# Forming T by pairs of 64-row matmuls in two PSUM banks, with the recurrence on the common bank pool

## The chip, the cores and the metric

One core of a Trainium2 chip. The metric is the device time of one launch in microseconds (us). Each call to the chip also ran the kernel before, so its median differs a little from call to call (1780.7 to 1785.0 us).

## The reference, cut to what matters

Two rounds of attention with a recurrent memory, each followed by a gated feed-forward layer. The sequence is cut into 64 segments of 32 tokens; each segment attends to itself and to 8 memory rows, and the memory of the next segment is the attention's output at those rows. So the 64 segments are a chain. B = 1, model width 448, 16 heads of 256.

```python
for s in range(n_seg):                       # 64 segments of 32
    h = jnp.concatenate([mem, xs], axis=1)   # 8 memory rows + 32 tokens
    q, k, v = h @ Wq, h @ Wk, h @ Wv         # (einsums over the heads, cut)
    p = _softmax(jnp.where(mask, q @ k * scale, -1e9))
    o = (p @ v) @ Wo
    mem = o[:, :M, :]
    outs.append(o[:, M:, :])
```

## The kernel before

Wq and Wk are merged ahead of time into one matrix M per head, so the scores are h · M · hᵀ. In every step the kernel forms T = Mᵀ · hᵀ: 56 blocks of 128 outputs, each a product over K = 448, which is 3.5 times the 128 rows that one matmul takes (128*128 in the page below). The kernel pads the last half with zeros and makes four passes. The two layers of the model run in one step, four segments apart, so a matmul of T has 2 x 40 = 80 columns. There are 68 steps; the first and last four have one layer and 40 columns.

```python
POOLS = {"R": [0, 1, 2, 3, 5]}               # bank 4 accumulates N and W_down, 6 and 7 belong to the recurrence

def t_unit(self, t, c, u0, m):               # a unit: m = 4, 5 or 6 blocks in one PSUM bank
    ...
    R = S.tile("R", 1)
    def mms():
        b = R.b()
        return [MM(b[:, j * n:j * n + n], S.M[:, kt, 16 * c + u0 + j, :],
                   S.hT[:, pp, s, kt, l0:l1, :].rearrange("p l x -> p (l x)"), start=(kt == 0), stop=(kt == 3))
                for j in range(m) for kt in range(4)]
    ...                                      # then copies of the bank to TTm (memory rows) and TTs (segment rows)

def s_mem(self, t):                          # memory scores: first step of the recurrence
    b = S.bC[0]                              # bank 6, fixed
    ...

class _Order:                                # a list scheduler fixes the order on all engines at build time
    ...
    if e == "pe" and o.mode != mode:         # it charges a change of array tiling 95 ns
        c += 95.0
```

The chain of a step is T, memory scores, softmax, P transposed, U, the product with N, and the new memory into hT. Behind it, segment scores (s_seg), U of the segment (u_seg, matmuls `PTs,hK`), the product with N (`Nw,big`) and the feed-forward layer (`xBT,big`, `big,hB`) fill TensorE.

## Time and profile before

| | before |
|---|---|
| median of the first 3 runs | 1780.73 us (1775.98 to 1781.08) |
| TensorE busy | 96% |
| T | 15232 matmuls, 546 us busy |
| granted TensorE clock, mean | 0.989 |

The groups by form split T into its two widths:

```profile
L127 PE MATMUL b<-hT,Mw 128*128 128x80 bf16 x13440 | 496.5, 202 | 3.6 <-DVE hT L685 3.6
...
L127 PE MATMUL b<-hT,Mw 128*128 128x40 bf16 x1792 | 49.5, 183 | 1.3 <-DVE hT L685 1.0 <-issue 0.3
```

The timeline of TensorE (start us, duration us, instruction, count, and in brackets the idle time before it) shows T as one block:

```profile
907.09 0.92 PE L127 MATMUL b<-Nw,big 128*128 128x448 bf16 x4
907.84 8.19 PE L127 MATMUL b<-hT,Mw 128*128 128x80 bf16 x224
915.87 0.92 PE L127 MATMUL b<-Nw,big 128*128 128x448 bf16 x4
...
928.55 0.17 PE L127 MATMUL b<-selm,lo 128*128 128x16 bf16 x1
929.20 0.36 PE L127 MATMUL b<-hi,seln 128*128 128x448 bf16 x1 [0.48 <-ACT hT L684]
```

224 matmuls take 8.19 us, 36 ns from start to start, and nothing in the block waits. The pause of 0.48 us before `hi,seln` is the recurrence waiting for ScalarE to empty bank 6. In two long windows of the steady state (us, then busy time of each engine, and the clock as PEclk):

```profile
100.00:900.00 800.00, 776.49 (x14338) 567.85 (x14335) 486.49 (x1384) 321.40 (x910) 33.59 (x61) 1.00 0.02 5
900.00:1700.00 800.00, 776.93 (x13901) 564.11 (x13899) 477.37 (x1341) 323.72 (x911) 35.61 (x64) 0.99 0.02 4
```

### The profile page before, as it was taken

The page shows a single profiled execution, that of the slowest core. Times are in us where ns is not written, and L with a number is a line of the kernel's source. Part 1 is how long each engine was busy: PE and PEld are TensorE (multiplying, and loading weights), DVE is VectorE, ACT ScalarE, POOL GpSimd, SP SyncE. Part 2 cuts the span into 40 slices and gives each one's busy share as a digit, 9 for nine tenths or more (in the row PEclk, how much of TensorE's full clock was granted, in tenths as well). Part 3 has the DMA queues.
Part 4 walks back from the last instruction along what each step waited for, and adds up shares of the span by engine and source line. Part 5 has one row for each costly group of instructions (what it writes and reads, how often), then busy time and mean ns, then how long its engine had stood idle before and what let it go on. Part 6 is the DMA issues. An engine that isn't in the chain of part 4 may idle for free.

```text
span 1780.3 us, 67770 instructions
## 1 busy us (share of the span) xinstructions
PE 1700.7 (96%) x30612; PEld 1226.7 (69%) x30612; DVE 1073.2 (60%) x3058; ACT 720.6 (40%) x2031; POOL 91.0 (5%) x156
## 2 busy tenths in 40 slices
PE   6899999999999999999999999999999999999997
PEld 2566766777677667767766776776677677667765
DVE  7647565565656556565655656565665656566554
ACT  5433433444443334444333444334344433434432
POOL 3000000000000000000000000000000000000000
PEclk9999999999999999999999999999999999999999
DMA  9700000000000000000000000000000000000000
GB/s 227 219 4 4 4 5 5 4 5 5 5 4 5 5 4 5 5 5 4 5 5 4 5 5 5 4 5 4 4 5 6 5 4 5 3 3 4 4 4 5
DMA packets 55760, 27.52 MB, mean 15 GB/s; under 512 B 44584, under 2 KB 54576, under 8 KB 55472
## 3 DMA queue, kind: packets, MB, share of 16 engines
q1 hardware_dynamic: 55120, 22.94, 5.3%
q8 instruction: 241, 3.95, 0.9%
q14 instruction: 47, 0.39, 0.1%
q10 hardware_dynamic: 352, 0.24, 0.1%
HBM read 10.33 MB, written 1.84 MB: 7 GB/s over the span
## 4 chain that ended last, share of the span: by engine, by line
PE 75%; DVE 6%; ACT 2%; issue 1%; DVEq 0%
PE b L127 75%; ACT big L684 1%; DVE big L685 1%; DVE stat L714 1%; DVE TTs L685 1%; DVE xn L721 1%; ACT hT L684 1%; DVE ys L1015 1%; DVE XA L1008 1%; DVE XB L968 0%; DVE Es L843 0%; DVE stat L842 0%; DVE TTm L685 0%; DVE hT L685 0%; DVE part L957 0%
## 5 line engine op out<-in xcount | busy, mean ns | idle before, releaser
L127 PEld LDWEIGHTS b<-hT,Mw 128*128 128x128 bf16 x15232 | 539.8, 100 | 25.3 <-DVE hT L685 11.2
L127 PE MATMUL b<-hT,Mw 128*128 128x80 bf16 (+1 forms) x15232 | 546.0, 200 | 5.0 <-DVE hT L685 4.6
L127 PE MATMUL b<-Nw,big 128*128 128x448 bf16 (+1 forms) x1936 | 394.9, 358 | 8.2 <-DVE big L685 5.6
L685 DVE CAST TTs<-b 128x320 bf16<-128x320 f32 (+5 forms) x574 | 261.3, 455 | 78.6 <-PE b L127 78.3
L127 PEld LDWEIGHTS b<-Nw,big 128*128 128x128 bf16 (+1 forms) x1936 | 163.7, 100 | 157.1 <-issue 21.5
L127 PE MATMUL b<-xBT,big 128*128 128x128 bf16 (+1 forms) x3808 | 219.6, 217 | 0.7 <-ACT xBT L684 0.7
L685 DVE CAST TTm<-b 128x80 bf16<-128x80 f32 (+5 forms) x580 | 134.7, 232 | 129.5 <-PE b L127 98.0
L127 PEld LDWEIGHTS b<-xBT,big 128*128 128x128 bf16 x3808 | 204.7, 98 | 2.4 <-ACT xBT L684 0.9
L127 PE MATMUL b<-Nw,UTm 128*32 128x448 bf16 x3752 | 192.0, 356 | 0.6 <-ACT UTm L684 0.6
L685 DVE CAST big<-b 128x512 bf16<-128x512 f32 (+1 forms) x190 | 121.3, 659 | 103.9 <-PE b L127 102.8
L684 ACT ACTIVATE big<-b 128x512 bf16<-128x512 f32 (+1 forms) x322 | 153.7, 525 | 48.2 <-PE b L127 45.0
L127 PEld LDWEIGHTS b<-Nw,UTm 128*32 128x32 bf16 x3752 | 95.2, 97 | 88.9 <-issue 18.7
L685 POOL COPY hK<-xn 32x448 bf16<-32x448 bf16 x136 | 75.6, 556 | 1521.6 <-DVE xn L721 1470.4
L684 ACT ACTIVATE TTs<-b 64x256 bf16<-64x256 f32 (+5 forms) x310 | 127.6, 412 | 29.6 <-PE b L127 22.4
L995 ACT ACTIVATE gT<-b 128x256 bf16<-128x256 f32 x226 | 86.4, 382 | 128.8 <-PE b L127 124.1
L684 ACT ACTIVATE TTm<-b 64x64 bf16<-64x64 f32 (+4 forms) x304 | 69.4, 228 | 159.4 <-PE b L127 152.5
L996 DVE TENSOR_TENSOR hB<-gT,b 128x256 bf16<-128x256 bf16 x226 | 93.6, 415 | 64.8 <-ACT gT L995 54.0
L896 ACT ACTIVATE hi<-b 128x448 bf16<-128x448 f32 x67 | 36.5, 544 | 193.7 <-PE b L127 193.5
L897 DVE TENSOR_TENSOR lo<-b,hi 128x448 bf16<-128x448 f32 x67 | 41.4, 619 | 121.2 <-ACT hi L896 121.2
L127 PE MATMUL b<-big,hB 128*128 128x448 bf16 (+1 forms) x476 | 107.3, 355 | 0.0
L684 ACT ACTIVATE hK<-b 8x448 bf16<-8x448 f32 x94 | 50.4, 536 | 122.5 <-PE b L127 121.0
L127 PE MATMUL b<-PTs,hK 40*128 40x512 bf16 (+1 forms) x640 | 86.4, 348 | 13.3 <-DVE XA L1008 7.1
(103 smaller groups left out, 1396.1 us busy)
## 6 DMA issues: line engine op xcount, KB each, us to landing
big<-in_A_Wo_dram SPq DMA_DIRECT2D x3, 896.0 KB, 5.8
out_dram<-ys SPq DMA_DIRECT2D x32, 56.0 KB, 1.9
big<-in_B_W_down_dram SPq DMA_DIRECT2D x1, 1568.0 KB, 6.8
XA<-in_A_x_dram SPq DMA_DIRECT2D x28, 56.0 KB, 2.0
big<-in_B_W_up_dram SPq DMA_DIRECT2D x1, 1344.0 KB, 8.1
big<-in_B_W_gate_dram SPq DMA_DIRECT2D x1, 1344.0 KB, 8.5
Nw<-in_A_Wo_dram SPq DMA_DIRECT2D x1, 896.0 KB, 6.4
XA<-in_A_x_dram ACTq DMA_DIRECT2D x4, 56.0 KB, 4.3
```

What stands on the lines that cost most here:

```text
L127: ins = E.matmul(out, lhsT=lhsT, rhs=rhs, **kw)
L684: return E.activation(out(), src(), ACT.Copy)
L685: return E.tensor_copy(out(), src())
L714: S.dve(lambda E: E.bn_stats(st[:, so:so + 6], x), D, rd, [(key, 0)])
L721: S.dve(lambda E, a=a, b=b, src=src: E.tensor_scalar(S.xn[:, i, a:b], src, st[:, so + 6:so + 7], st[:, so + 8:so + 9], op0=ALU.subtract, o ...
L896: S.act(lambda E: E.activation(S.hi[:, :], b[:, 0:D], ACT.Copy), D, S.ps(6), [("hi",)])
L897: S.dve(lambda E: E.tensor_tensor(S.lo[:, :], b[:, 0:D], S.hi[:, :], ALU.subtract), D, S.ps(6) + [("hi",)], [("lo",)])
L995: S.act(lambda E, k=k, R=R, n=n: E.activation(S.gT[:, k % 2, 0:n], R[0].b()[:, 0:n], ACT.Relu), n, R[0].res(), [("gT", k % 2)])
L996: S.dve(lambda E, k=k, R=R, n=n, fcs=fcs: E.tensor_tensor(S.hB[:, fcs[0]:fcs[-1] + 1, 0:w], S.gT[:, k % 2, 0:n].rearrange("p (a b) -> p a ...
L1008: S.dve(lambda E: E.tensor_tensor(S.XA[64:128, q % 4, :], S.bO[0:64, 0:D], S.XB[0:64, p % 2, :], ALU.add), D, S.ps(4, half=(0,)) + xb, [(" ...
L1015: S.dve(lambda E: E.tensor_tensor(S.ys[64:128, p % 2, :], S.bO[64:128, 0:D], S.XB[64:128, p % 2, :], ALU.add), D, S.ps(4, half=(1,)) + xb, ...
```

## The change

Intent: the last half pass wastes half of the array. Two blocks, A and B, are formed together in two banks. Matmuls of 64 rows run as pairs, the upper half of the array on one bank, the lower half on the other: in a first part the upper halves of A's passes beside the lower halves of B's, and A's last half beside B's; in a second part the halves exchange banks. That is seven pairs for two blocks, 3.5 passes per block. A wait on TensorE's own counter keeps the second part from meeting the first in the same bank. Such pairs need more banks, so the recurrence gives up banks 6 and 7, and everything except bank 4 comes from one pool of seven.

```diff
-    POOLS = {"R": [0, 1, 2, 3, 5]}
+    POOLS = {"R": [0, 1, 2, 3, 5, 6, 7]}
...
-        self.M = self.sb("Mw", [128, 4, NO, 128])
+        self.M = self.sb("Mw", [128, 3, NO, 128])
+        self.M3 = self.sb("M3", [128, NO // 2, 128])
...
+                for j in range(m):
+                    v = slice(j * n, j * n + n)
+                    if not second:
+                        for kt in range(3):
+                            out.append(MM(a[:, v], S.M[top, kt, oa + j, :], mov(kt, top), start=(j == kt == 0), stop=False))
+                            out.append(MM(b[:, v], S.M[bot, kt, ob + j, :], mov(kt, bot), start=(j == kt == 0), stop=False))
+                        out.append(MM(a[:, v], S.M3[top, slot0 + j, :], mov(3, top), start=False, stop=False))
+                        out.append(MM(b[:, v], S.M3[bot, slot0 + j, :], mov(3, bot), start=False, stop=False))
+                    else:
+                        for kt in range(3):
+                            e = j == m - 1 and kt == 2
+                            out.append(MM(b[:, v], S.M[top, kt, ob + j, :], mov(kt, top), start=False, stop=e))
+                            out.append(MM(a[:, v], S.M[bot, kt, oa + j, :], mov(kt, bot), start=False, stop=e))
...
+            S.mm(mms, (3 if second else 4) * m * S.pitch(n), rd + rd2 if second else rd,
+                 R[0].res() + R[1].res() + (...), mode=1)
...
-        b = S.bC[0]
+        C = S.tile("R", 1)                   # s_mem, and likewise p_t_mem, u_mem, un_mem, m_t, m_nat
```

More of the change, by code (lines that the diff above doesn't have):

```diff
@@ L119, in pe @@
         waits = self._need("pe", reads, writes)
+        done = max([self.lastw[r][1] for r in reads if r[0] == "done"], default=0)
+        if self.known["pe"].get("pe", 0) < done:
+            self.known["pe"]["pe"] = done
+            waits.append((ev.sem, done))
         ev.n += 1
@@ L432, in alloc @@
         self.banks = [b[:, :] for b in bank]
-        self.bO, self.bC = bank[4], bank[6:8]
+        self.bO = bank[4]
     @staticmethod
@@ L547, in setup @@
         S.dve(lambda E: E.tensor_scalar(S.ident[:, :], cf[:, 0:128], 0.0, None, op0=ALU.is_equal), 128, [("Sm",)], [("ident",)])
-        S.pool(lambda E: E.memset(S.M[64:128, 3, 0:28, :], 0.0), 1800, (), [("Mz", 0)])
-        S.dve(lambda E: E.memset(S.M[64:128, 3, 28:56, :], 0.0), 1800, (), [("Mz", 1)])
         for j in range(4):
@@ L599, in setup @@
                 u, r = i + 8 * odd, slice(64 * odd, 64 * odd + 64)
-                S.cp(lambda u=u: S.M[0:64, 3, u:48:16, :], lambda T=T, r=r: T.b()[r, 0:384].rearrange("p (c x) -> p c x", c=3), 384,
-                     T.res(half=(odd,)), [("M", 3, u)])
-                S.cp(lambda i=i, odd=odd: S.M[0:64, 3, 48 + i, 64 * odd:64 * odd + 64], lambda T=T, r=r: T.b()[r, 384:448], 64,
-                     T.res(half=(odd,)), [("M", 3, 48 + i, odd)])
-        S.Mkeys = [("M", kt, u) for kt in range(4) for u in range(16)] + [("M", kt, 48 + i, o) for kt in range(4) for i in range(8) for o in range(2)]
-        S.Mkeys += [("Mz", 0), ("Mz", 1)]
+                for c in range(4):
+                    side, slot = S.PLACE[16 * c + (u if c < 3 else i)]
+                    d, w, x = 64 * side, (128 if c < 3 else 64), (64 * odd if c == 3 else 0)
+                    S.cp(lambda d=d, w=w, x=x, slot=slot: S.M3[d:d + 64, slot, x:x + w],
+                         lambda T=T, r=r, c=c, w=w: T.b()[r, 128 * c:128 * c + w], w, T.res(half=(odd,)), [("M3", c, u)])
+        S.Mkeys = [("M", kt, u) for kt in range(3) for u in range(16)] + [("M", kt, 48 + i, o) for kt in range(3) for i in range(8) for o in range(2)]
+        S.Mkeys += [("M3", c, u) for c in range(4) for u in range(16)]
         S.Nkeys = [("N", o) for o in range(NO)]
@@ L751, in ln_b, with t_pass @@
         S.cp(lambda: S.xBT[:, :, :].rearrange("p a b -> p (a b)"), lambda: T.b().bitcast(BF)[:, 0:512], 512, T.res(), [("xBT",)])
-    def t_unit(self, t, c, u0, m):
+    def t_pass(self, t):
         S = self
@@ L760, in t_unit @@
         n = nl * KEYS
-        R = S.tile("R", 1)
-        def mms():
-            b = R.b()
-            return [MM(b[:, j * n:j * n + n], S.M[:, kt, 16 * c + u0 + j, :],
-                       S.hT[:, pp, s, kt, l0:l1, :].rearrange("p l x -> p (l x)"), start=(kt == 0), stop=(kt == 3))
-                    for j in range(m) for kt in range(4)]
-        rd = [("hTx", pp, s)] + S.mkeys(pp, s, l0, l1)
-        if t == 0:
-            rd = rd + S.Mkeys
-        dst = [(nm, c, u0, half) for nm in ("TTm", "TTs") for half in ((0, 1) if c == 3 else (0,))]
@@ L773, in t_unit, with part, mms @@
-        S.mm(mms, 4 * m * S.pitch(n), rd, R.res() + dst)
-        src = lambda: R.b()[:, 0:m * n].rearrange("p (o l x) -> p o l x", o=m, l=nl)
+        rd = [("hTx", pp, s)] + S.mkeys(pp, s, l0, l1) + (S.Mkeys if t == 0 else [])
+        top, bot = slice(0, 64), slice(64, 128)
+        mov = lambda kt, h: S.hT[h, pp, s, kt, l0:l1, :].rearrange("p l x -> p (l x)")
+        keys = lambda c, u0: [(nm, c, u0, half) for nm in ("TTm", "TTs") for half in ((0, 1) if c == 3 else (0,))]
+        def part(g, R, second):
+            A, B = S.PAIRS[g]
+            m = A[2]
+            slot0 = sum(x[0][2] for x in S.PAIRS[:g])
+            oa, ob = 16 * A[0] + A[1], 16 * B[0] + B[1]
+            def mms():
+                a, b = R[0].b(), R[1].b()
+                out = []
+                for j in range(m):
[11 more added lines that the diff above has]
+                            out.append(MM(a[:, v], S.M[bot, kt, oa + j, :], mov(kt, bot), start=False, stop=e))
+                return out
+            rd2 = [("done", g)]
+            S.mm(mms, (3 if second else 4) * m * S.pitch(n), rd + rd2 if second else rd,
+                 R[0].res() + R[1].res() + ([("order",)] if second else keys(*A[:2]) + keys(*B[:2]) + [("done", g), ("order",)]), mode=1)
+            if second:
+                for k, T in zip((A, B), R):
+                    S.t_copies(t, T, *k)
@@ L775, in t_unit, with t_copies @@
+        R = []
+        for g in range(len(S.PAIRS)):
+            R.append([S.tile("R", 1), S.tile("R", 1)])
+            part(g, R[g], False)
+            if g:
+                part(g - 1, R[g - 1], True)
+        g = len(S.PAIRS) - 1
+        part(g, R[g], True)
+    def t_copies(self, t, R, c, u0, m):
+        S = self
+        l0, l1 = S.layers(t)
+        nl = l1 - l0
+        src = lambda: R.b()[:, 0:m * nl * KEYS].rearrange("p (o l x) -> p o l x", o=m, l=nl)
         for half in ((0, 1) if c == 3 else (0,)):
@@ L784, in t_unit @@
                  lambda h=h: src()[h, :, :, 0:SEG], m * nl * SEG, rr + z, [("TTs", c, u0, half)])
-    UNITS = [(3, 0, 4), (3, 4, 4)] + [(c, u, m) for c in range(3) for u, m in ((0, 6), (6, 5), (11, 5))]
-    TKEYS = [(c, u, half) for c, u, m in UNITS for half in ((0, 1) if c == 3 else (0,))]
+    PAIRS = [((3, 0, 4), (3, 4, 4)), ((0, 0, 6), (1, 0, 6)), ((0, 6, 5), (0, 11, 5)), ((1, 6, 5), (1, 11, 5)), ((2, 6, 5), (2, 11, 5)),
+             ((2, 0, 3), (2, 3, 3))]
+    TKEYS = [(k[0], k[1], half) for pair in PAIRS for k in pair for half in ((0, 1) if k[0] == 3 else (0,))]
+    PLACE = {}
+    for _a, _b in PAIRS:
+        for _j in range(_a[2]):
+            PLACE[16 * _a[0] + _a[1] + _j] = (0, len(PLACE) // 2)
+            PLACE[16 * _b[0] + _b[1] + _j] = (1, (len(PLACE) - 1) // 2)
     def s_mem(self, t):
@@ L793, in s_mem @@
         nl = l1 - l0
-        b = S.bC[0]
-        S.mm(lambda: [MM(b[:, l * KEYS:l * KEYS + KEYS], S.TTm[:, c, l, :], S.hT[:, pp, s, c, l, :], start=(c == 3), stop=(c == 2))
+        C = S.tile("R", 1)
+        S.mm(lambda: [MM(C.b()[:, l * KEYS:l * KEYS + KEYS], S.TTm[:, c, l, :], S.hT[:, pp, s, c, l, :], start=(c == 3), stop=(c == 2))
                       for l in range(l0, l1) for c in (3, 0, 1, 2)], 100.0 * nl,
-             [("TTm",) + k for k in S.TKEYS] + [("hTx", pp, s)] + S.mkeys(pp, s, l0, l1), S.ps(6))
+             [("TTm",) + k for k in S.TKEYS] + [("hTx", pp, s)] + S.mkeys(pp, s, l0, l1), C.res())
         st = S.stat
-        src = b[:, l0 * KEYS:l1 * KEYS].rearrange("p (l x) -> p l x", l=nl)
+        src = lambda: C.b()[:, l0 * KEYS:l1 * KEYS].rearrange("p (l x) -> p l x", l=nl)
         bc = lambda a: st[:, a:a + nl].unsqueeze(2).to_broadcast([128, nl, KEYS])
@@ L802, in s_mem @@
         n = nl * KEYS
-        S.dve(lambda E: E.tensor_reduce(st[:, 32:32 + nl], src, AX.X, ALU.max), n, S.ps(6), [("sm", 0)])
-        S.dve(lambda E: E.tensor_tensor(Em, src, bc(32), ALU.subtract), n, S.ps(6) + [("sm", 0)], [("Em",)])
+        S.dve(lambda E: E.tensor_reduce(st[:, 32:32 + nl], src(), AX.X, ALU.max), n, C.res(), [("sm", 0)])
+        S.dve(lambda E: E.tensor_tensor(Em, src(), bc(32), ALU.subtract), n, C.res() + [("sm", 0)], [("Em",)])
         S.act(lambda E: E.activation(Fm, Em, ACT.Exp, scale=SCALE), n, [("Em",)], [("Fm",)])
@@ L857, in p_t_mem @@
         S = self
-        pT = S.bC[1][:, :].bitcast(BF)
-        S.mm(lambda: [MM(pT[:, 0:128], S.Pm[:, :], S.ident[:, :], is_transpose=True)], 60.0, [("Pm",), ("ident",)], S.ps(7))
-        S.cp(lambda: S.PTm[:, :], lambda: pT[:, 0:128], 128, S.ps(7), [("PTm",)])
+        C = S.tile("R", 1)
+        pT = lambda: C.b().bitcast(BF)
+        S.mm(lambda: [MM(pT()[:, 0:128], S.Pm[:, :], S.ident[:, :], is_transpose=True)], 60.0, [("Pm",), ("ident",)], C.res() + [("PTm",)])
+        S.cp(lambda: S.PTm[:, :], lambda: pT()[:, 0:128], 128, C.res(), [("PTm",)])
     def u_mms(self, l, c, pp, s, ps, PT, w):
@@ L874, in u_mem @@
         l0, l1 = S.layers(t)
-        S.mm(lambda: [m for c in range(4) for l in range(l0, l1) for m in S.u_mms(l, c, pp, s, S.bC[l][:, c * 128:], S.PTm, 8)], 350.0,
+        C = {l: S.tile("R", 1) for l in range(l0, l1)}
+        S.mm(lambda: [m for c in range(4) for l in range(l0, l1) for m in S.u_mms(l, c, pp, s, C[l].b()[:, c * 128:], S.PTm, 8)], 350.0,
              [("PTm",)] + [("hKx", pp, s, l) for l in range(l0, l1)] + [("hKm", pp, s, l) for l in range(l0, l1)],
-             S.ps(*[6 + l for l in range(l0, l1)]), mode=1)
+             [r for l in C for r in C[l].res()] + [("UTm", l) for l in C], mode=1)
         for l in range(l0, l1):
-            S.cp(lambda l=l: S.UTm[:, 0:NO, l * 8:l * 8 + 8], lambda l=l: S.bC[l][:, 0:D].rearrange("p (o q) -> p o q", o=NO), D,
-                 S.ps(6 + l), [("UTm", l)], eng=("act", "dve") if l1 - l0 == 1 else (("act", "dve")[l],))
+            S.cp(lambda l=l: S.UTm[:, 0:NO, l * 8:l * 8 + 8], lambda l=l: C[l].b()[:, 0:D].rearrange("p (o q) -> p o q", o=NO), D,
+                 C[l].res(), [("UTm", l)], eng=("act", "dve") if l1 - l0 == 1 else (("act", "dve")[l],))
     def un_mem(self, t):
         S = self
-        b = S.bC[0]
+        C = S.tile("R", 1)
         def mms():
@@ L891, in mms @@
                     lhs = S.UTm[:, o:o + 2, :].rearrange("p a q -> p (a q)")
-                    out.append(MM(b[32 * j:32 * j + 32, 0:D], lhs, S.N[:, o, :], start=(k == 0), stop=(k == 13)))
+                    out.append(MM(C.b()[32 * j:32 * j + 32, 0:D], lhs, S.N[:, o, :], start=(k == 0), stop=(k == 13)))
             return out
-        S.mm(mms, 14 * S.pitch(D) + 100.0, [("UTm", 0), ("UTm", 1)] + (S.Nkeys if t == 0 else []), S.ps(6), mode=2)
-        S.act(lambda E: E.activation(S.hi[:, :], b[:, 0:D], ACT.Copy), D, S.ps(6), [("hi",)])
-        S.dve(lambda E: E.tensor_tensor(S.lo[:, :], b[:, 0:D], S.hi[:, :], ALU.subtract), D, S.ps(6) + [("hi",)], [("lo",)])
+        S.mm(mms, 14 * S.pitch(D) + 100.0, [("UTm", 0), ("UTm", 1)] + (S.Nkeys if t == 0 else []), C.res() + [("hi",), ("lo",)], mode=2)
+        S.act(lambda E: E.activation(S.hi[:, :], C.b()[:, 0:D], ACT.Copy), D, C.res(), [("hi",)])
+        S.dve(lambda E: E.tensor_tensor(S.lo[:, :], C.b()[:, 0:D], S.hi[:, :], ALU.subtract), D, C.res() + [("hi",)], [("lo",)])
     def m_t(self, t):
@@ L904, in m_t @@
         l0 = max(l0, S.layers(t + 1)[0])
-        b1, b0 = S.bC[1], S.bC[0]
+        C = S.tile("R", 1)
         sel = [("sel", j) for j in range(4)]
-        S.mm(lambda: [MM(b1[:, c * 16:c * 16 + 16], x[:, c * 128:c * 128 + 128], S.selm[:, :], start=(i == 0), stop=(i == 1))
-                      for c in range(3) for i, x in enumerate((S.hi, S.lo))], 150.0, [("hi",), ("lo",)] + sel, S.ps(7))
-        S.mm(lambda: [MM(b0[:, 448:464], x[:, 320:448], S.selm[:, :], start=(i == 0), stop=(i == 1)) for i, x in enumerate((S.hi, S.lo))],
-             50.0, [("hi",), ("lo",)] + sel, S.ps(6))
-        w = [("hTm", pp, s, l) for l in range(l0, l1)]
-        S.cp(lambda: S.hT[:, pp, s, 0:3, l0:l1, SEG:KEYS], lambda: b1[:, 0:48].rearrange("p (c l q) -> p c l q", c=3, l=2)[:, :, l0:l1, :],
-             48, S.ps(7), w, eng=("dve",))
-        v = b0[64:128, 448:464].rearrange("p (l q) -> p l q", l=2)[:, l0:l1, :]
-        for half in range(2):
-            S.cp(lambda half=half: S.hT[64 * half:64 * half + 64, pp, s, 3, l0:l1, SEG:KEYS], lambda: v, 16, S.ps(6, half=(1,)),
-                 [("hTm3", pp, s, half)], eng=("act",))
+        mk = S.mkeys(pp, s, l0, l1)
+        S.mm(lambda: [MM(C.b()[:, c * 16:c * 16 + 16], x[:, w:w + 128], S.selm[:, :], start=(i == 0), stop=(i == 1))
+                      for c, w in ((0, 0), (1, 128), (2, 256), (3, 320)) for i, x in enumerate((S.hi, S.lo))], 200.0,
+             [("hi",), ("lo",)] + sel, C.res() + mk)
+        v = lambda: C.b()[:, 0:64].rearrange("p (c l q) -> p c l q", c=4, l=2)[:, :, l0:l1, :]
+        S.cp(lambda: S.hT[:, pp, s, 0:3, l0:l1, SEG:KEYS], lambda: v()[:, 0:3], 48, C.res(), mk[:-2], eng=("dve",))
+        S.cp(lambda: S.hT[0:64, pp, s, 3, l0:l1, SEG:KEYS], lambda: v()[64:128, 3], 16, C.res(half=(1,)), mk[-2:-1], eng=("act",))
+        S.cp(lambda: S.hT[64:128, pp, s, 3, l0:l1, SEG:KEYS], lambda: v()[64:128, 3], 16, C.res(half=(1,)), mk[-1:], eng=("act",))
     def m_nat(self, t):
@@ L922, in m_nat @@
         pp, s = (t // 2) % 2, t % 2
-        b0 = S.bC[0]
-        S.mm(lambda: [MM(b0[:, 0:D], S.seln[:, :], x[:, :], start=(i == 0), stop=(i == 1)) for i, x in enumerate((S.hi, S.lo))],
-             2 * S.pitch(D), [("hi",), ("lo",), ("sel",)] + [("sel", j) for j in range(4)], S.ps(6))
-        for l in range(*S.layers(t)):
-            if l == 1 and t == LAG:
-                continue
+        C = S.tile("R", 1)
+        ls = [l for l in range(*S.layers(t)) if not (l == 1 and t == LAG)]
+        S.mm(lambda: [MM(C.b()[:, 0:D], S.seln[:, :], x[:, :], start=(i == 0), stop=(i == 1)) for i, x in enumerate((S.hi, S.lo))],
+             2 * S.pitch(D), [("hi",), ("lo",), ("sel",)] + [("sel", j) for j in range(4)], C.res() + [("hKm", pp, s, l) for l in ls])
+        for l in ls:
             r = slice(64 * l + 32, 64 * l + 40)
-            S.cp(lambda r=r: S.hK[r, pp, s, :], lambda r=r: b0[r, 0:D], D, S.ps(6, half=(l,)), [("hKm", pp, s, l)])
+            S.cp(lambda r=r: S.hK[r, pp, s, :], lambda r=r: C.b()[r, 0:D], D, C.res(half=(l,)), [("hKm", pp, s, l)])
     def u_seg(self, t):
@@ L1027, in step @@
             S.m_nat(t)
-        for k in S.UNITS:
-            S.t_unit(t, *k)
+        S.t_pass(t)
         if not last:
```

## The prediction

> **What bounds the kernel now.** TensorE. The page's busy table gives PE 96% of 1780.3 us, DVE 60%, ACT 40%; the chain that ended last is 75% PE. In both 800 us windows of the steady state PE is busy 776 us. PE time saved there is time saved, unless it turns into a wait.
>
> **What T costs now.** The groups by form show 13440 matmuls of 128 rows x 80 columns, 496.5 us, and 1792 of 40 columns, 49.5 us: 546 us, 31% of the span. The timeline shows them back to back, one start every 36 ns, 224 per step, 8.19 us, without a wait inside.
>
> **What the change removes.** Per output block 3.5 instead of 4 passes: 11760 pairs of half-array matmuls instead of 13440 full ones, and 1568 instead of 1792. This needs both of a pair to run, and to load weights, side by side. The trace has such pairs already: the 40-row matmuls of hK with PTm at 128 columns start 2 to 4 ns apart and the pairs follow every 56 ns, the pace of one full matmul of that width. After a fresh load of both weights the second pair is again 3 ns apart, so I take the two loads to be parallel. Estimate: 1680 x 36 ns + 224 x 27 ns = 66 us saved.
>
> **What it adds.** Row-paired T is another array tiling than the surrounding full-array work. [...] over a change of tile shape the next matmul ends about N/2.4 + 106 ns after the last (159 ns at N=128, 294 at 448, 319 at 512; 700 such places), so about 103 ns lost each. The instruction order of the built kernels has 721 such changes before and 1189 after: T is broken into islands by 128-row work. 468 x 103 ns = 48 us back.
>
> Matmul instructions of T rise from 15232 to 26656 plus as many loads, four instructions per 36 ns. Evacuation work of T is unchanged, but arrives two banks at a time.
>
> **Common pool.** The recurrence no longer reuses banks 6 and 7: today PE idles 0.65 us in 32 places between the selection matmuls (lo with selm) and hi with seln, 20.5 us in all, until ACT has emptied the shared bank. With another bank that goes, mostly filled by other work: -10 to -15 us. Against it T holds up to six of seven banks, so some new waits on evacuation: +5 us.
>
> **Sum.** 1780.7 - 66 + 48 - 12 + 5 = 1755 us. Range 1715 to 1800. Faster by over 2%: 0.36; within: 0.50; slower: 0.14.
>
> **What would show each step.** T pairs starting every 36 ns, total T busy near 480 us; matmul starts inside a pair 2 to 4 ns apart; about 1190 tile-shape changes at about 103 ns; the 0.65 us waits before hi/seln gone.
>
> **What would make it wrong.** (1) Two 64-row weight loads could share one path. Full loads with 40-column matmuls pace at 25 ns (TTs with hT[...]). If that floor holds for each half, a pair takes 50 ns and T grows by some 120 us: time near 1900. (2) Instruction supply: twice the instructions per T microsecond. (3) New waits for banks, or for PE's own completion before the second half of a pair, making T wait on evacuation. (4) The other way: interleaving also fills idle time.

The 48 us rest on the 700 measured places; N/2.4 is the slope of the three points beside it, (319 - 159) / (512 - 128) = 0.417 ns per column. The 25 ns "floor" is the pace that the trace before shows: matmuls of 40 columns (TTs with hT) start 25 ns apart, where the slope gives 17 ns for 40 columns. That two loads share one path was a fear, and the +5 us for new waits a guess from no number of the trace.

## More of the kernel before

Times are medians over the runs of a kernel.

From the page: busy times and instruction counts per engine; the granted clock in 40 slices, in tenths; the instruction queue (packets, MB, share); the chain that ended last; and T's matmuls (count, busy us, mean ns of one, idle before).

```profile
PE 1700.7 (96%) x30612; PEld 1226.7 (69%) x30612; DVE 1073.2 (60%) x3058; ACT 720.6 (40%) x2031; POOL 91.0 (5%) x156
...
PEclk9999999999999999999999999999999999999999
...
q8 instruction: 241, 3.95, 0.9%
...
PE 75%; DVE 6%; ACT 2%; issue 1%; DVEq 0%
...
L127 PE MATMUL b<-hT,Mw 128*128 128x80 bf16 (+1 forms) x15232 | 546.0, 200 | 5.0 <-DVE hT L685 4.6
```

TensorE is the limit (96% busy, 75% of the chain that ended last), and the clock is nearly always full (mean 0.989).

## The result, and the profile after

The changed kernel takes 1963.39 us (median of 4 runs, 1954.52 to 1965.91), against 1780.9 for the kernel before: ratio 1.1016, 95% interval 1.0969 to 1.1063. A ratio here is the mean time of one kernel's fast runs over that of the other's of the same rounds, so it is not quite the ratio of the medians. The prediction of 1755 us was wrong by more than its range and in sign.

The same lines of the page after (T is now two groups, because its last half pass reads another tensor, M3, shown as `M`):

```profile
PE 1770.4 (90%) x42036; PEld 1239.8 (63%) x42036; DVE 1002.2 (51%) x2966; ACT 769.4 (39%) x2290; POOL 92.7 (5%) x155
...
PEclk9879989999999999999999999999989999999888
...
q8 instruction: 331, 5.42, 1.2%
...
PE 82%; DVE 10%; issue 6%; ACT 3%; POOL 0%; DVEq 0%; ACTq 0%; POOLq 0%
...
L131 PE MATMUL b<-hT,Mw 64*128 64x80 bf16 (+1 forms) x22848 | 571.7, 204 | 90.5 <-issue 66.9
...
L131 PE MATMUL b<-hT,M 64*128 64x80 bf16 (+1 forms) x3808 | 328.9, 208 | 6.5 <-issue 6.5
```

TensorE is less busy (90%) and the total of its busy time is larger; the clock row has eights and sevens; instruction packets rose from 241 to 331. The two long windows:

```profile
100.00:900.00 800.00, 733.10 (x17859) 521.29 (x17863) 409.85 (x1216) 311.62 (x925) 33.49 (x57) 0.94 0.02 5
900.00:1700.00 800.00, 739.18 (x17630) 521.91 (x17622) 411.32 (x1201) 313.78 (x920) 33.27 (x56) 0.96 0.02 5
```

The mean clock is 0.94 to 0.96 there. What TensorE waited for, summed over the span (us in total, times, longest):

```profile
PE b L131 <- issue: 81.4, 77, 5.1
PE b L131 <- DVE Es L893: 34.8, 28, 1.2
PE b L131 <- DVE hT L689: 21.9, 30, 0.8
```

"issue" is time in which the engine waited for nothing that the profile shows: 81.4 us, against 6.1 us before. The list of the kernel before has no wait on `Es`, and little on hT:

```profile
PE b L127 <- issue: 6.1, 6, 3.3
...
PE b L127 <- DVE hT L685: 4.6, 15, 1.0
```

The timeline of one pair of steps after has all the symptoms:

```profile
597.72 0.39 PE L131 MATMUL b<-PTs,hK 40*128 40x512 bf16 x2 [0.28 <-DVE stat L719]
599.36 0.43 PE L131 MATMUL b<-PTs,hK 40*64 40x256 bf16 x4 [1.24 <-DVE Es L893]
...
600.97 0.38 PE L131 MATMUL b<-hT,Mw 64*128 64x80 bf16 x6 [0.58 <-DVE hT L689]
...
601.21 0.40 PE L131 MATMUL b<-hT,Mw 64*128 64x80 bf16 x6
...
601.48 0.40 PE L131 MATMUL b<-hT,Mw 64*128 64x80 bf16 x6
...
606.69 0.27 PE L131 MATMUL b<-hT,Mw 64*128 64x80 bf16 x6
...
606.83 0.27 PE L131 MATMUL b<-hT,Mw 64*128 64x80 bf16 x6
...
608.51 0.56 PE L131 MATMUL b<-hT,Mw 64*128 64x80 bf16 x22
610.19 0.42 PE L131 MATMUL b<-hT,Mw 64*128 64x80 bf16 x14 [1.12 <-issue]
...
626.55 0.55 PE L131 MATMUL b<-Nw,big 128*128 128x448 bf16 x2
```

First there are 1.24 us and 0.58 us of waiting before T, on VectorE. Then T starts slowly: from 601.21 to 601.48 eight matmuls (four pairs, of which the fence shows the first six) take 0.27 us, 67 ns per pair. At 606.69 it is twice as fast, eight in 0.14 us, about 36 ns per pair. Then it stops for 1.12 us with no releaser. In the next step T is cut into islands by `Nw,big`. The windows over the same stretch show the clock:

```profile
595.80:599.20 3.40, 2.03 (x33) 0.87 (x29) 3.25 (x9) 2.36 (x7) 0.00 (x0) 1.00 0.07 17
599.20:606.00 6.80, 6.07 (x160) 5.54 (x162) 3.53 (x13) 3.48 (x10) 2.38 (x4) 0.50 0.01 2
606.10:609.00 2.90, 2.90 (x164) 2.84 (x158) 1.36 (x4) 1.20 (x4) 0.00 (x0) 1.00 0.03 6
609.05:610.15 1.10, 0.02 (x2) 0.00 (x0) 0.00 (x0) 0.00 (x0) 0.00 (x0) 1.00 0.00 0
```

In the 3.4 us of the gap TensorE is busy 2.03 us at full clock (busy counts each matmul's whole span, for T some 200 ns where the starts are 36 ns apart; streaming, counted as below, is estimated at about 1.2 us); the next 6.8 us, with T inside, run at 0.50; after that the clock is full again. In the last window no engine has work: TensorE is stopped by nothing that the profile shows.

From the starts in the trace, three things can be counted:

- **The pace of a pair.** At full clock and 80 columns the mean is 36.0 ns over 19440 starts, the two halves usually 3 to 4 ns apart. So the pairs do run side by side, at the pace of one full matmul.
- **The 70 stalls in T.** I counted gaps of more than 300 ns between two TensorE instructions of T where the second waits for no other engine, from 60 us after the start: 70, 82 us in all. If all instructions of TensorE in the trace are numbered in order (its loads, its matmuls and its 856 semaphore and drain instructions), all 70 stalls fall on a number with remainder 193 modulo 256. Without the 856 they do not. The instruction queue's packets are 16384 bytes, and 256 instructions of TensorE go by for each (331 packets, 84928 instructions). Each stall ends about 1.4 us after such a packet has landed; from 60 us on the closest two packets landed 3.3 us apart.
- **The clock.** The granted clock changes in steps of 3.41 us between 1.0 and 0.5. Counted from 60 us on to about 20 us before the end, 65 such stretches are at 0.5 after and 9 before. A drop is a full-clock stretch followed by one at 0.5. Of the 43 drops after, 42 follow a stretch in which the matmuls' own streaming filled less than 1.5 us of the 3.41. (Streaming is an estimate from the trace: 0.42 ns per column, the slope between a start every 56 ns at 128 columns and every 189 ns at 448; matmuls that run side by side count once.) Counted so in the twelve readable traces, 275 of 278 drops follow less than 1.5 us, while only 28 of 5672 full-clock stretches that no drop follows have so little.

### The profile page after: what moved, and what is told of

Read it like the earlier page. It is cut to its first block, busy times and chain, and to the rows that moved or that the text cites. A ratio compares the mean times of both kernels' runs of the same rounds, so it can differ in the third digit from the quotient of the medians.

```text
span 1963.6 us, 91234 instructions
## 1 busy us (share of the span) xinstructions
PE 1770.4 (90%) x42036; PEld 1239.8 (63%) x42036; DVE 1002.2 (51%) x2966; ACT 769.4 (39%) x2290; POOL 92.7 (5%) x155
## 4 chain that ended last, share of the span: by engine, by line
PE 82%; DVE 10%; issue 6%; ACT 3%; POOL 0%; DVEq 0%; ACTq 0%; POOLq 0%
PE b L131 82%; DVE xn L725 1%; DVE big L689 1%; DVE lo L949 1%; DVE ys L1064 1%; DVE hK L689 1%; DVE XA L1057 1%; ACT hi L948 1%; ACT PTs L688 1%; DVE Es L893 1%; DVE hT L689 1%; DVE stat L895 1%; DVE stat L892 1%; DVE stat L718 0%; ACT TTm L688 0%
## 5 line engine op out<-in xcount | busy, mean ns | idle before, releaser
L131 PE MATMUL b<-hT,Mw 64*128 64x80 bf16 (+1 forms) x22848 | 571.7, 204 | 90.5 <-issue 66.9
L131 PEld LDWEIGHTS b<-hT,Mw 64*128 64x128 bf16 x22848 | 529.4, 102 | 183.5 <-issue 100.8
L131 PE MATMUL b<-Nw,big 128*128 128x448 bf16 (+1 forms) x1936 | 413.7, 364 | 0.5 <-DVE ys L1007 0.4
L131 PE MATMUL b<-hT,M 64*128 64x80 bf16 (+1 forms) x3808 | 328.9, 208 | 6.5 <-issue 6.5
L689 DVE CAST TTm<-b 128x80 bf16<-128x80 f32 (+6 forms) x502 | 103.8, 222 | 331.7 <-PE b L131 327.1
L688 ACT ACTIVATE TTm<-b 128x80 bf16<-128x80 f32 (+6 forms) x450 | 95.0, 226 | 406.6 <-PE b L131 406.4
L131 PEld LDWEIGHTS b<-hT,M 64*128 64x128 bf16 x3808 | 208.9, 105 | 4.5 <-issue 4.5
L689 DVE CAST TTs<-b 128x320 bf16<-128x320 f32 (+5 forms) x506 | 208.8, 427 | 4.4 <-PE b L131 4.3
L688 ACT ACTIVATE TTs<-b 128x320 bf16<-128x320 f32 (+5 forms) x446 | 170.3, 397 | 13.7 <-PE b L131 6.4
L689 DVE CAST big<-b 128x512 bf16<-128x512 f32 (+1 forms) x164 | 102.2, 625 | 126.1 <-PE b L131 125.0
L131 PE MATMUL b<-PTs,hK 40*128 40x512 bf16 (+1 forms) x640 | 86.0, 356 | 48.8 <-DVE Es L893 34.8
```

What stands on the lines that cost most here:

```text
L131: ins = E.matmul(out, lhsT=lhsT, rhs=rhs, **kw)
L688: return E.activation(out(), src(), ACT.Copy)
L689: return E.tensor_copy(out(), src())
```

## The experiments

The theory to test: the change costs time in four ways that have nothing to do with the pace of the pairs: instruction supply, half clock after gaps, drains at changes of the array's tile shape, and new waits. "Drain" below is a name for the about 103 ns lost at a change of shape, and "instruction supply", "fetch" or "page" for the stalls at remainder 193 modulo 256; the traces show the lost time, not what goes on in it. The first expectations take their figures from the trace after: 70 stalls, 82 us; 65 half-clock stretches, at most 65 x 3.41 / 2 = 111 us; 470 more changes x 103 ns = 48 us; 34.8 us of waiting on `Es`. Rivals: half-array matmuls themselves are slow or count as low activity for the clock; or the common pool is to blame. Four kernels give a wrong T on purpose (named so below). They still passed the comparison with the reference, so T's share of the output lies within its tolerance. "Right result" below therefore means that the edit keeps T right by construction and that the run passed.

| run | median us | ratio to before | mean clock | half-clock stretches | stalls in T | shape changes |
|---|---|---|---|---|---|---|
| before | 1780.9 to 1785.0 | 1 | 0.989 | 9 | 1 | 700 |
| after | 1963.4 | 1.1016 | 0.939 | 65 | 70, 82 us | 1170 |
| pool_only | 1764.0 | 0.9888 | 0.994 | 5 | 0 | 643 |
| pairs_own_banks | 2111.1 | 1.1853 | 0.949 | 60 | 17, 12 us | 1299 |
| order_full_array (wrong T) | 1795.8 | 1.0069 | 0.955 | 45 | 1 | 672 |
| pairs_half_instr (wrong T) | 1885.5 | 1.0567 | 0.937 | 66 | 14, 23 us | 1170 |
| full_array_warmed (wrong T) | 1748.1 (3 fast runs) | 0.9803 | 0.994 | 3 | 1 | 703 |
| pairs_warmed | 1942.5 | 1.0883 | 0.976 | 24 | 93, 113 us | 1201 |
| hybrid_2_groups | 1964.0 | 1.1006 | 0.964 | 38 | 0 | 947 |
| hybrid_3_groups | 1850.3 | 1.0380 | 0.970 | 31 | 1 | 1140 |
| full_array_more_drains (wrong T) | 1984.8 | 1.1125 | 0.937 | 70 | 0 | 2282 |
| pool_only_split_columns | 1989.8 | 1.1148 | 0.994 | 5 | 41, 24 us | 643 |

The last three columns are counted in the traces from 60 us on, half-clock stretches to about 20 us before the end (the trace of full_array_warmed is that of its second run, see there). A single stall of about 0.4 to 1.2 us in a column is a gap that the same rule catches.

### pool_only: the pool alone

```diff
 # kernel before, T in four full passes
-    POOLS = {"R": [0, 1, 2, 3, 5]}
+    POOLS = {"R": [0, 1, 2, 3, 5, 6, 7]}
-        b = S.bC[0]
+        C = S.tile("R", 1)      # s_mem, p_t_mem, u_mem, un_mem, m_t, m_nat as in the changed kernel
```

> The common pool alone, with T in four full passes as before. Main theory (the 183 us are instruction-fetch stalls about 80 us, half-clock windows about 100 us, drains about 48 us, new waits about 30 us, less 66 us of T): the pool does no harm by itself; 1765 to 1790 us, granted clock 0.98 or more, no stall of T inside its stream. Rival (the shared pool makes the new waits, and these the half clock): 1820 us or more and clock 0.96 or less.

Measured: 1763.96 us, ratio 0.9888 (0.9873 to 0.9904), clock 0.994, right result, 1 us under the expected range. The pool is not to blame; it is the good half of the change, and this version beats both kernels, by 1.1% over the kernel before, which is clear of noise but within the 2% that the verdict calls the same.

### pairs_own_banks: the pairs alone

```diff
 # changed kernel
-    POOLS = {"R": [0, 1, 2, 3, 5, 6, 7]}
+    POOLS = {"R": [0, 1, 2, 3, 5]}
-        C = S.tile("R", 1)
+        b = S.bC[0]             # the six functions as before
```

> T by row pairs, but the recurrence keeps banks 6 and 7 and T works from five banks. Rival (the pool makes the waits): half-clock windows nearly gone, clock 0.98 or more, time about 1830 us, fetch stalls still 80 us or more. Main theory, in which row pairs and the order they bring are to blame: 1930 us or more, clock 0.95 or less, fetch stalls still there, tile-shape changes about 1300 instead of 1170.

Measured: 2111.06 us, ratio 1.1853, clock 0.949. TensorE's waits:

```profile
PE b L131 <- DVE TTs L689: 131.9, 181, 1.2
PE b L131 <- DVE Es L893: 54.0, 28, 1.9
```

With five banks T waits for its own copies (131.9 us). The wait on `Es` that opens the gap before T is there without the shared pool too, so the pool doesn't make it; it comes with the order that the pairs bring. The stalls of supply fell to 12 us, where both theories had expected them to stay. That the waits for banks gave the fetch time to catch up is the author's guess; no run tests it.

### order_full_array: same order, no row pairs

```diff
 # changed kernel; each pair becomes one matmul of 128 rows, alternately into bank a and bank b (wrong T)
-   MM(a, S.M[top, kt, oa + j, :], mov(kt, top)), MM(b, S.M[bot, kt, ob + j, :], mov(kt, bot))
+   MM(d, S.M[:, kt, o + j, :] or S.M3[:, slot0 + j, :], S.hT[:, pp, s, kt, l0:l1, :])    # (o, d) = (oa, a), (ob, b) in turn
```

The scheduler still counts the parts as row pairs, so the order of all other instructions on TensorE, VectorE and ScalarE is identical to the changed kernel's.

> Wrong result on purpose: same order, banks and copies as the changed kernel, but each pair of half-array matmuls is one full 128-row matmul, so half the instructions and no tile-shape change at T. Fetch stalls 0, drains of T gone. If the half clock comes from waits of the order (main theory): clock stays 0.94 to 0.96, time 1963 - 82 - 48 = about 1830 us. If it comes from half-array matmuls counting as low activity (rival): clock 0.985 or more and about 1730 us.

Measured: 1795.76 us, ratio 1.0069, clock 0.955, 45 half-clock stretches.

```profile
PE b L131 <- DVE Es L887: 34.8, 28, 1.2
...
PE b L131 <- issue: 4.2, 3, 2.6
```

Stalls and extra drains are gone (1 gap and 672 shape changes counted), and the clock still falls (0.955). So it is the order, not half-array matmuls, that brings most of the half clock (45 stretches of 65); that its gaps do it is tested by full_array_warmed. I had expected 1830 us from adding the costs; the rest is taken up below.

### pairs_half_instr: row pairs with fewer instructions

```diff
 # changed kernel; two blocks share one pair of 160 columns (the moving operand reads two kt at once; wrong T)
-                for j in range(m):
-                    v = slice(j * n, j * n + n)
+                for j in range(0, m, 2):
+                    w = min(2, m - j)
+                    v = slice(j * n, (j + w) * n)
```

> Wrong result on purpose: row pairs as in the changed kernel, same order, banks and copies, but two blocks share one pair of 160-column matmuls, so 4/7 of T's matmuls and loads with the same streaming time. Main theory: the T stalls at instruction-page boundaries (70, 82 us) vanish, 1870 to 1900 us, clock unchanged near 0.94. If the stalls are not instruction supply but PE's own semaphore waits or bank waits: they stay, about 1960 us.

Measured: 1885.51 us, ratio 1.0567, clock 0.937.

```profile
PE b L131 <- DVE Es L897: 34.8, 28, 1.2
PE b L131 <- issue: 29.7, 17, 5.6
```

56 of the 70 stalls vanish. All 14 that remain, 23 us, lie in the steps with one layer at the two ends, where the edit did not apply. In the trace the other instructions of TensorE, VectorE and ScalarE stand in the same order as in the changed kernel, so the stalls were instruction supply. The gain of 78 us holds up to 15 us of another kind: one 160-column pair takes 69 ns by the pace of this trace, two of 80 take 72.

### full_array_warmed: useless work in the gaps

```diff
 # order_full_array, plus full-array matmuls of 448 columns into bank 4 while it holds nothing (wrong T)
+   6 x MM(bank 4, N[:, 0, 0:128], N[:, 0, :])     # before the u_seg matmuls of c = 3, even steps
+   2 x MM(bank 4, N[:, 0, 0:128], N[:, 0, :])     # before the first part of T, even steps
```

> Run order_full_array again (wrong result on purpose, same order), with useless full-array matmuls of 448 columns put into the two gaps where PE waits before every second T: six before the last segment matmuls (31 places), two before T (32 places), 47 us of added PE work in all. Main theory (a 3.4 us clock window with too little matmul work makes the next ones half speed; the gaps do it): half-clock windows 45 -> under 15, clock 0.955 -> 0.985 or more, and the time falls although work is added: 1795 -> 1715 to 1750 us. Rival (the half clock does not come from these gaps): clock stays near 0.955 and the time stays or grows, 1795 to 1840 us.

Measured: 1748.12 us, the median of the three fast runs, ratio 0.9803 (0.9786 to 0.9821, so unclear at the 2% mark), clocks of 0.991 to 0.996. The fourth, which was the profiled one, was slow from start to end (3272.92 us, no clock records; matmuls of 448 columns mostly started 417 ns apart instead of 189) and is left out; why is not known. I ran the kernel once more for a readable trace:

> The same kernel as full_array_warmed, once more, only because the profiled execution of that run was a half-speed outlier (3271 us, no clock records) and so its trace can't be read. Expected: about 1750 us, clock 0.99 or more, half-clock windows under 15 against 45 in order_full_array, the waits of TensorE before the last segment matmuls nearly gone from its list of waits.

Measured: 1746.34 us, clock 0.994, 3 half-clock stretches. The waits of TensorE in this trace:

```profile
PE b L131 <- DVE hT L722: 12.5, 30, 0.7
...
PE b L131 <- issue: 3.6, 2, 2.7
```

The wait on `Es` is no longer in the list, because TensorE is doing useless work there. The kernel does about 250 more matmuls and is 48 us faster than order_full_array. That shows the gaps at work: the order of everything else is the same in both kernels. The gain was at the low end of what I expected, and less than the 42 half-clock stretches could be worth (an estimate: 42 x 3.41 / 2 = 72 us). Why was not taken apart; the useless matmuls before T do not hold it up, since in nearly all places T starts 57 to 59 ns after the copy into hT that it waits for, as without them.

### pairs_warmed: the same in the changed kernel

```diff
 # changed kernel, plus the same useless matmuls in the same places
```

> The changed kernel itself (right result) with the same useless matmuls in the same gaps. Main theory: clock 0.94 -> 0.97 or more, gain of 50 to 90 us from the clock, part of which comes back as more instruction-page stalls in T, because T at full speed asks for instructions faster: 1880 to 1920 us, stall time up from 82 us. Rival: 1960 us or more.

Measured: 1942.50 us, ratio 1.0883, clock 0.976. A miss: 21 us gained, where 1880 to 1920 us would have been 43 to 83.

```profile
PE b L131 <- issue: 110.6, 103, 5.3
```

The clock came back as expected (65 half-clock stretches to 24, worth 41 x 3.41 / 2 = 70 us if all of that had been streaming), but T at full speed outruns the supply more: 93 stalls and 113 us, all again at remainder 193. So part of the clock's gain came back as stalls, and the two faults hide each other: at half clock T had asked for less, a pair every 67 ns in the stretch shown of the changed kernel, 60 instructions per us, against 111 at 36 ns. The 31 us of added stalls do not cover the whole miss; the rest stays open.

### full_array_more_drains: the cost of a change of shape

```diff
 # order_full_array, but the first matmul of each of T's 12 parts per step is a row pair (wrong T)
+                        if j == kt == 0:
+                            out.append(MM(a[:, v], S.M[top, 0, oa, :], mov(0, top), ...))
+                            out.append(MM(b[:, v], S.M[bot, 0, ob, :], mov(0, bot), ...))
+                            continue
```

> Run order_full_array (1796 us, 672 tile-shape changes; wrong result on purpose) with the first matmul of each of T's 12 parts per step made a row pair: about 1600 more shape changes, hardly any half-array work, no more than a few extra instructions. If the 90 us between order_full_array and pairs_half_instr are mostly drains at shape changes of about 103 ns each: 1796 + 165 = 1940 to 2000 us. If they come from half-array matmuls as such (slower, or counted as low activity by the clock), this run stays under 1850 us.

Measured: 1984.77 us, ratio 1.1125, 2282 shape changes, clock 0.937. 1610 more changes cost 189 us, 117 ns each. From a row pair to a full matmul of T the ends are 142 ns apart instead of 36, so the change itself costs 106 ns; and the clock lost 25 more stretches. The drops are about as many (33, against 32 in order_full_array), but more stretches at 0.5 follow on another one (37 against 13), so the clock comes back later. Half-array work is almost nil here, so the rival (half-array matmuls as such) is not needed for the 90 us between order_full_array and pairs_half_instr. The traces speak against it too: pairs start at the pace of full matmuls (36.0 ns), and of 68 full-clock stretches of the changed kernel that are filled mostly with T's pairs (over 80% of at least 2 us of streaming) not one was followed by half clock.

### pool_only_split_columns: supply without row pairs

```diff
 # pool_only; each T matmul of 80 columns as two of 40, one per layer (right result)
-            return [MM(b[:, j * n:j * n + n], S.M[:, kt, ...], S.hT[:, pp, s, kt, l0:l1, :], ...) for j in range(m) for kt in range(4)]
+            return [MM(b[:, j * n + i * KEYS:j * n + i * KEYS + KEYS], S.M[:, kt, ...], S.hT[:, pp, s, kt, l0 + i, :], ...)
+                    for j in range(m) for i in range(nl) for kt in range(4)]
```

> Run pool_only (1764 us; right result, no tile-shape change added) with each 80-column matmul of T split into two of 40: 896 T instructions per step at one start per 25 ns, 80 instructions per us instead of 56. Streaming grows by 13440 x (50 - 36) = 188 us. If instruction supply is a limit of its own (one page of 256 TensorE instructions per 3.4 to 4.0 us in the changed kernel's stalls, so 64 to 75 per us), stalls appear inside T at the same remainder of the instruction count modulo 256, 20 to 100 us in all: 1970 to 2060 us. If the stalls need row pairs: none, 1950 us.

Measured: 1989.82 us, ratio 1.1148, right result, clock 0.994.

```profile
PE b L127 <- issue: 26.3, 48, 1.9
```

Full-array matmuls stall too: 41 times, all at remainder 193 modulo 256, when T asks for 80 instructions per us. Where two of these stalls come one packet of 256 instructions apart (9 times), the second ends 3.6 to 4.2 us after the first, about 62 to 72 instructions per us; T of pool_only asks for two per 36 ns, 56 per us, and has no stall. The row pairs ask for four instructions every 36 ns, 111 per us.

### hybrid_2_groups and hybrid_3_groups: an attempt at a better version

```diff
 # changed kernel; kt = 0..2 by full-array matmuls, only the last half pass by row pairs, collected per group of pairs
+    GROUPS = ((0, 1, 2), (3, 4, 5))        # hybrid_2_groups: six banks per group
+    GROUPS = ((0, 1), (2, 3), (4, 5))      # hybrid_3_groups: four banks per group
```

> A version without the three costs: common pool, T with three full-array passes per block and only the last half pass by row pairs, all pairs of six banks in one go, so two tile-shape excursions per step and no more matmul instructions than before (4 per block). Theory: no page stalls; T saves 66 us against pool_only (1764), four shape changes per step at 103 ns cost 28 us: 1726 us, plus waits for banks, since six of seven banks fill before any is emptied: 1725 to 1780 us. If bank waits dominate: above 1790 us.

Measured: 1964.04 us, ratio 1.1006.

```profile
PE b L131 <- DVE TTm L689: 40.4, 62, 0.8
PE b L131 <- DVE Es L888: 34.7, 28, 1.2
PE b L131 <- DVE TTs L689: 33.1, 32, 1.1
PE b L131 <- DVE hK L689: 30.0, 30, 1.0
```

> As hybrid_2_groups but with four banks per group and six shape changes per step (42 us): 1740 us if banks are no limit, 1735 to 1775 us. If shape changes cost more than the 103 ns each, or draw in other work between (more changes than 6 per step), above 1780 us.

Measured: 1850.26 us, ratio 1.0380, clock 0.970, 1140 shape changes.

Both give right results and have no supply stalls to speak of, and both lose to pool_only and missed their ranges (1725 to 1780 and 1735 to 1775 us). With six banks held until the last pass, T and what follows wait for copies (40.4 us for `TTm`, 33.1 us for `TTs`). With four, there are 497 more shape changes than in pool_only, about 7 per step, and the gap before T with its half clock is there again (34.8 us of waiting on `Es`, 31 half-clock stretches). My sum for them had left out what the order does to the gaps, for the second time.

## Why the prediction was wrong

The runs give a ledger in differences of medians, from after back to before:

| from | to | us | what it holds |
|---|---|---|---|
| after 1963.4 | pairs_half_instr 1885.5 | 78 | instruction supply (up to 15 us of it the wider matmul) |
| pairs_half_instr | order_full_array 1795.8 | 90 | row pairs' 498 shape changes: 498 x 103 ns = 51 us of drain; the 14 stalls left, 23 us; and 21 half-clock stretches, at most 21 x 3.41 / 2 = 36 us |
| order_full_array | full_array_warmed 1748.1 | 48 | half clock after the order's gaps |
| full_array_warmed | before 1784.95 | -37 | the saved passes and the pool, less the waits that remain |

Point by point:

- **"1680 x 36 ns + 224 x 27 ns = 66 us saved": right as streaming time.** Pairs start every 36.0 ns at full clock with the halves 3 to 4 ns apart, as read from the `PTm,hK` pairs of the trace before. The feared 50 ns pair did not occur. What a busy table would show as T (572 + 329 us) is no contradiction: it holds T at half clock, and spans that overlap (204 and 208 ns in the mean, a pair every 36 ns).
- **"468 x 103 ns = 48 us back": right, and too small.** 470 more changes were counted, each about 103 to 106 ns (in full_array_more_drains 142 ns from end to end instead of 36). The term missed that added changes can cost clock as well: in full_array_more_drains a change cost 117 ns on average, and the half-clock stretches went from 45 to 70.
- **"Matmul instructions of T rise from 15232 to 26656 plus as many loads, four instructions per 36 ns": the step that failed first.** The prediction named it and gave it no microseconds. The edit of pairs_half_instr took 59 us of stalls away and 78 us of time, and the stalls of the changed kernel come to 82 us in all. The numbers for it were in the trace before: 256 TensorE instructions per packet, and the packets' times. All 218 counted stalls (70 + 14 + 93 + 41) fall at remainder 193 modulo 256. They came where T asks for 80 or more instructions per us (111 for pairs of 80 columns; about 160 in the steps with one layer, where pairs of 40 columns start every 25 ns), and none at 56 (the single one of the kernel before, 0.5 us at the same remainder, fell at 84.0 us, in a step with one layer, where T's matmuls start 25 ns apart).
- **"-12" and "+5" for the pool and new waits: the step that failed second.** The pool by itself gave more than that (about 20 us), and the wait before `hi,seln` went away in pool_only as predicted; it had been 14.9 us in the list of waits, not 20.5 (the 0.65 us of the prediction is from start to start, the idle time 0.48). But the new waits were larger, 34.8 us on `Es` and 21.9 us on hT (4.6 before) against 5 us forecast, and they were summed as waits. They fell together before T into a stretch with little matmul work (42 of 43 drops follow under 1.5 us of streaming in 3.41), and the clock mostly halved for one or two stretches of 3.41 us, with T, at full clock a pair every 36 ns, inside them (65 such stretches against 9; filling the gaps gave back 48 us in the order without pairs). The kernel before was close to that edge already: in its steady state it dropped about once every 310 us, each time after a stretch with just over 1.4 us of streaming.
- **What would make it wrong, (2) and (3), came true.** The listed guess of near 1900 us for (1) was near the result for a reason that was not the real one.

One thing stays open: of the 90 us between pairs_half_instr and order_full_array, the split between drain, stalls and clock is an estimate from counts, not a run; its parts add up to more than 90 (51 + 23 + 36 = 110), and the 36 us are an upper bound, as if matmuls had filled every half-clock stretch. How much of the 37 us at the end is waiting was not taken apart either.

The wait that opens the gap has this cause. On VectorE the segment softmax stands in the queue behind other work (timeline of VectorE after):

```profile
597.37 0.21 DVE L689 CAST hT<-b 128x48 bf16<-128x48 f32 x1
...
598.07 0.62 DVE L689 CAST hK<-b 8x448 bf16<-8x448 f32 x1
598.72 0.49 DVE L893 TENSOR_TENSOR Es<-b,stat 128x320 f32<-128x320 f32 x1
```

`Es` is the last reader of a score bank. It starts at 598.72, after a copy of 0.62 us for the memory rows, and the segment matmuls that were given that bank wait for it until 599.36. The scheduler plans with its own durations and may not have seen it coming; its plan was not looked at. That the order, not the pool, brings it is shown by pool_only and pairs_own_banks.

## What to carry to other kernels

Count instructions per microsecond as well as columns per microsecond: here splitting T's matmuls in two left the pace of a pair at 36.0 ns and raised the demand from 56 to 111 instructions per us, and the sign of what that cost was 70 stalls with no releaser, 82 us, at a fixed remainder modulo 256. Before you trust a few hundred nanoseconds of added waiting, look at whether they fall together just ahead of dense work; gaps of 1.24 and 0.58 us close together cost here, by estimate, up to another 1.7 us (3.41 / 2) for each of the one or two half-clock stretches that followed. And take a change of two parts apart before judging it: here the small part (the pool) was worth 1.1%, and the large part cost 11% on top of it.
